# Mask products before or after the score products, chosen by what TensorE ran last

## The chip, the cores and the metric

The kernel runs on one core of a Trainium2 chip. The metric is the device time of one execution, in microseconds (us); lower is better. A core has five engines that work side by side and meet through semaphores: PE (TensorE, matrix products), DVE (VectorE), ACT (ScalarE), POOL (GpSimd) and SP (SyncE, which here issues the DMA transfers). The profile has a sixth column, PEld: the loads of the stationary operand, which overlap PE's products.

## The reference

Two attentions follow each other. The first has 8 batches of 8 heads, 576 positions, 64 features, and keeps only the 32 largest scores of each row:

```python
scores = scale * np.matmul(q, k.transpose(0, 1, 3, 2))
kth = np.partition(scores, -top_k, axis=-1)[..., -top_k:-top_k + 1]
scores = np.where(scores >= kth, scores, -1000000000.0)
attn = softmax(scores)                      # with 1e-9 added to the sum
x = np.matmul(attn, v)                      # heads side by side: (8, 576, 512)
```

The second (the MoE stage) takes `x`, picks 2 of 4 experts for each position by a gate, and lets each expert do a causal attention with its own projections:

```python
q, k, v = x @ wq[e], x @ wk[e], x @ wv[e]
a = softmax(where(causal, -1e9, scale * (q @ k.T)))
out += gate[:, e] * (a @ v @ wo[e])
```

## The kernel before

**Tiling.** Two heads form a pair, so a batch is four pairs and the program has 32 of them. The 2 x 576 query rows of a pair are cut into nine tiles of 128 rows, numbered `j`: 0 to 3 belong to the first head (operands `opa`), 5 to 8 to the second (`opb`), and tile 4 holds the 64 left-over rows of each.

**The first attention.** For each group of three tiles PE makes the scores (`scores`, float32r products, L554), ACT copies them to SBUF (`copy`, tile `s`, L558), and DVE finds the 32 largest of each row in a chain of maxima (`f1` to `f5`, `win`, `rep`, L568 to L609). ACT then makes a mask from the scores and the 32nd value (`mask`, bf16, L649): zero for what is kept, positive for what isn't. `stats` (L674) turns the row's maximum and its sum into four rows of numbers; PE transposes them (`s8`, tile `stat`, L723) and ACT writes them into the operands (`s9`, L727).

Then the scores are made a second time, transposed, with keys on the partitions. This is the task `st` (L752). It has two parts that add up in one PSUM tile of two banks: `product` makes four float32r products (128 x 128 stationary; 256 and 320 columns, twice), the second pair of which reads the extended operand `k2a` or `k2b`; then `piece` multiplies each of five mask tiles with a bf16 matrix that holds a huge negative number on its diagonal (`negi`), which pushes the scores that are not kept far down. There are eight such tasks in a pair, and a ninth, `j == 4`, with eight products and ten or eleven mask pieces. ACT takes the exponential (`exp`, tile `pt`, L799), and PE multiplies the result with the values (`av`, L769): float32 products whose stationary operand is only 64 columns wide, two side by side in the array. The first product of a PSUM bank is issued with `start=True`, the others add to it.

**The MoE stage** of a batch runs spread out between the pairs of the following batch: projections (`proj`, `vproj`, float32r), scores for five row tiles (`s_stage`, L1015), a row maximum on DVE (`m_stage`), the exponential on ACT (`e_stage`), transposes on PE (`t_stage`, L1048), the product with the values (`avm`), and the output projection (`prod`). For the first four row tiles, `s_stage` first puts the causal mask into PSUM (`identb` and `tri`, bf16, full array), then adds three pairs of products `qk` whose contraction has 64 rows, two side by side.

**Order of issue.** No engine's order is written by hand. Every piece of work is added to a `Plan` as a task with an engine, an estimated duration, its predecessors, its buffers and a priority. `Plan.order` (L144) plays the tasks through: for each engine it takes, among the tasks whose estimated start lies within `SLACK` nanoseconds of the earliest, the one with the smallest priority, and advances that engine's clock. The priority is a due number, counted in pairs, plus a constant for the task's name (`BIAS`) and an offset for its stage (`D_...`). The program is issued in the order that comes out. Rings of buffers bound how far the engines run apart: three PSUM tiles (`SLOT`), one accumulator (`ACC`), 14 masks, one `raw`.

PE's tasks also have a kind (L99). The plan carries one flag, `short`, which says how the last PE task ended:

```python
            if t.kind:
                if short and t.kind not in (SHORT, TURN):
                    dur += self.SWITCH
                t.first = short
                short = t.kind in (SHORT, MIXED) or t.kind == EITHER and not short
```

`SWITCH` is 107 ns. `LONG` is float32r work (scores, projections), `SHORT` is float32 work and transposes (`av`, `avm`, `t_stage`, `s8`, `c4`). In the kernel before, `st` is `MIXED` (starts with float32r, ends with bf16), `s_stage` is `TURN` for the first four row tiles; no task is `EITHER`, and `t.first` is set but read by nobody.

Of the kernel before, what the change touches and what calls it, by code (L numbers as in the profile page):

```python
# [19 lines left out]
P = 128  # L20
TOPK = 32
OFF = (0, 64)
BASE = (0, 64)
# [75 lines left out]
LONG, SHORT, EITHER, MIXED, TURN = 1, 2, 3, 4, 5  # L99


class Plan:
# [5 lines left out]
           ("POOL", "SP"): 1400.0, ("DVE", "SP"): 1400.0, ("PE", "SP"): 1400.0}  # L108

    PORT = ("f1", "f3", "f4", "s1", "s7", "ot", "constants", "sub", "low_again")  # L110
    SLACK = 48.1507
    GAP = 160.0


# [123 lines left out]
def pool(n):  # L238
# [2 lines left out]

PEF = 1.0

BIAS = {"<lambda>": 21.16406, "again": 7.086664, "av": 0.291422, "avm": 7.96669, "c1": 6.060996, "c2": -16.917509, "c3":
        -25.219518, "c4": 7.40449, "c5": -35.33028, "cast": 16.673692, "cast_swap": -11.231639, "check1":
        -20.549209, "check2": 47.362819, "check3": -38.010145, "compare": 10.37121, "constants": 3.77208,
        "copy": -5.244973, "count": 19.276636, "diag": 12.150313, "dup": -0.574571, "dup1": -16.263021, "dup2":
# [4 lines left out]
        "load_swap": -1.709559, "loadv": -1.18649, "low_again": -15.590234, "m_stage": -34.500069, "mark":  # L252
        10.382567, "mask": -4.199012, "neg": 9.127403, "neg2": -15.174664, "o_stage": -15.926681, "oh":
        -11.134218, "ol": 20.300811, "ot": -22.486721, "prod": 24.66927, "proj": 0.24706, "rep": -3.538618,
        "s1": -38.259631, "s2": -18.732471, "s3": -11.549524, "s4": -14.828572, "s6": -6.937403, "s7": 7.577078,
        "s8": -2.208531, "s9": -18.824699, "s_stage": 0.053481, "scores": -0.261279, "st": -0.017376, "store":
        -19.029398, "sub": 10.142028, "t_stage": -1.573227, "tails": 9.736612, "vproj": 1.204296, "win":
        18.47031, "xh": 7.127005, "xl": 10.21211}
D_K2 = 29.144853
D_PREP = 2.849825  # L260
D_SC = 0.543928
D_TIE = 11.578646
D_MASK = 1.607309
D_STAT = -3.592427
D_TAIL = 0.282302
D_STEP = 0.102808
D_MOE = 4.208214
D_LAST = 5.999043
D_PEN = 4.17838
D_SPAN = 4.144087  # L270
MP = (14,3)
STO = (0, 1, 5, 2, 6, 3, 7, 8, 4)

# [2 lines left out]
def kernel(ctx, tc, qk, vL, wq, wk, wv, wo, out):  # L276
# [13 lines left out]
    def mm(o, l, r, start=False, stop=False):  # L290
        nc.tensor.matmul(o, l, r, start=start, stop=stop, skip_group_check=True)  # L291
# [107 lines left out]
    pl = Plan()  # L399
    add = pl.add  # L400
    lo, hi, al = slice(0, 64), slice(64, 128), slice(0, 128)
# [30 lines left out]
    def parts_of(j):  # L432
        return [(x, REST[x]) for x in range(2)] if j == 4 else [rows_of(j)]
# [80 lines left out]
        w.v = add("SP", 910, lambda: nc.sync.dma_start(w.vt.t, vL[b, i]), bufs=[w.vt], prio=3, tag="loadv")  # L514
        return w

    def product(sl, o0, split, ops, ls, rs, stop):

        k = 0
        for x, r, t in ops:  # L520
            for l, rr in zip(ls, rs):
                for c0, c1 in halves(split):
                    mm(sl[:, o0 + c0:o0 + c1], t[l][:, r], t[rr][:, OFF[x] + c0:OFF[x] + c1], start=(k == 0),
                       stop=stop and k == 2 * len(ops) - 1)
                k += 1
# [218 lines left out]
    def tail(w, shift, xb):  # L744
        acc = Buf(ACC)

        def piece(sl, prt, o0, split, c0, c1, lhsT, r):
            for a, z in ((c0, min(c1, split)), (max(c0, split), c1)):
                if a < z:
                    mm(sl[prt, o0 + a:o0 + z], lhsT, negi[:, r + a - c0:r + z - c0])  # L750

        def st(j, sl):  # L752
            split = SPLIT[0] if j < 4 else SPLIT[1]
            o0 = 512 - split
            product(sl.t, o0, split, parts(w, j), (1, 3), (0, 2), False)
            for x, r in parts_of(j):
                if j == 4:
                    prt = slice(64 * x, 64 * x + 64)
                    kc = slice(512, 576) if x == 0 else slice(0, 64)
                else:  # L760
                    prt = al
                    kc = slice(r.start - OFF[x], r.stop - OFF[x])
                c0 = 512 if x == 0 else 0
                piece(sl.t, prt, o0, split, c0, c0 + 64, w.mask[4].t[:, kc], 64 * x)
                for t in range(4):
                    c0 = BASE[x] + t * P
                    piece(sl.t, prt, o0, split, c0, c0 + P, w.mask[t + 5 * x].t[:, kc], 0)

        def av(j, pts):  # L769
            v = w.vt.t  # L770
# [13 lines left out]
        for j in STO:  # L784
            pl.due = w.p + D_TAIL + D_STEP * len(es)
            sl = Buf(SLOT)
            pt = ptb[j] = Buf(PT)
            x = 0 if j < 4 else 1
            o0 = 512 - (SPLIT[0] if j < 4 else SPLIT[1])
            need = [shift[x], w.k2d[x]] + (w.masked[0:5] if j < 4 else w.masked[4:9])  # L790
            if j == 4:
                need = shift + w.masked + w.k2d
            elif j > 4:
                need.append(shift[0])
            mb = w.mask if j == 4 else (w.mask[0:5] if j < 4 else w.mask[4:9])
            a = add("PE", 767 if j != 4 else 1500, lambda j=j, sl=sl: st(j, sl), need, bufs=[sl, pt] + used(w, j, True) + mb, prio=2, tag="st",
                    kind=MIXED)
            w.last_st.append(a)
            es[j] = add("ACT", act(S), lambda sl=sl, pt=pt, o0=o0: nc.scalar.activation(  # L799
                pt.t, sl.t[:, o0:o0 + S], AF.Exp, scale=0.125), [a], bufs=[sl, pt], prio=1, tag="exp")  # L800
        a = None
        for j in (0, 1, 2, 3, 4):
# [3 lines left out]
            a = add("PE", 1020 if j != 4 else 790, lambda j=j, pts=pts: av(j, pts), [es[k] for k in jj] + [w.v, a],  # L806
                    bufs=pts + [acc, w.vt], prio=1, tag="av", kind=SHORT)
# [6 lines left out]
        a = add("PE", 250, neg, [c], bufs=[acc, xb], prio=1, kind=LONG)  # L814
# [8 lines left out]
    def moe(b, p, xbs, xdone, wd, span, final):  # L823
        v = nc.vector
        v2, gg, ot = Buf(V2), Buf(G), Buf(OT)
# [39 lines left out]
        for t in range(5):  # L865
            sl = Buf(SLOT)
# [93 lines left out]
        for gp in range(2):  # L960
# [6 lines left out]
            for name, k in (("q", 0), ("k", 2)):  # L967
                sl = Buf(SLOT)
                o0 = 512 - 288
# [41 lines left out]
            for t in (0, 1, 2, 3, 4):  # L1011
# [3 lines left out]
                def s_stage(t=t, w=w, sl=sl, qk=qk, bd=bd):  # L1015
                    qh, ql, kh, kl = qk.t
                    if t < 4:
                        for h in range(2):
                            mm(sl.t[:, 512 * h + t * P:512 * h + w], identb, tri, start=True)
                        for n, (l, rr) in enumerate(((qh, kh), (ql, kh), (qh, kl))):  # L1020
                            for h in range(2):
                                r = slice(64 * h, 64 * h + 64)
                                mm(sl.t[:, 512 * h:512 * h + w], l[r, t * P:(t + 1) * P], rr[r, 0:w], stop=(n == 2))
# [47 lines left out]
                a = add("ACT", n * act(w, True, 1, 1), e_stage, [a], bufs=[sl, sm, pr], prio=2)  # L1071
                exps.append(a)
# [64 lines left out]
        split = []  # L1137
# [74 lines left out]
    t = add("PE", 100, check2, [t], bufs=[fin])  # L1212
    add("DVE", 100, check3, [t], bufs=[fin])
    for t in pl.order():
        t.fn()


    again = nc.values_load(flag, min_val=0, max_val=1)
    with tc.If(again > 0):
        for x in range(2):  # L1220
            blank(nc.vector, x, 0)
        blank_later()
        marks.clear()
        with tc.For_i(0, B) as b:
            pl.restart()
            batch(b, 0, {n: [] for n in "vqko"}, True)
            for t in pl.order():
                t.fn()


# [42 lines left out]
```

## Time and profile before

| what | value |
|---|---|
| time, median of 3 runs | 1211.62 us (1210.65 to 1213.2) |
| time of the profiled execution | 1211.31 us |
| its span, first to last instruction | 1209.5 us |
| granted TensorE clock, mean | 0.976 |
| PE busy | 1125.3 us, 93% of the span |
| DVE busy | 1096.4 us, 91% |
| ACT busy | 986.6 us, 82% |
| POOL busy | 378.4 us, 31% |

A row of the profile names a line of the kernel, an engine, an operation, and the tiles it writes and reads, `out<-in`, with the shape. All of `mm`'s products have the line L291, so the tiles tell them apart: `slot<-opa,opa` is a score product, `slot<-opa,k2a` the second pair of a `st`, `slot<-negi,mask` a mask product, `acc<-pt,vt` is `av`, `slot<-tri,identb` the causal mask, `slot<-qk,qk` the MoE scores. In the timeline a row begins with the start and the length of a run of such instructions, ends with their count, and has in square brackets how long the engine was idle before it and whose work ended that. PE's products are pipelined: the next begins before the one before has ended, so lengths overlap, and the distance from one start to the next is what a product takes of PE's time.

### The profile page before, as it was taken

How to read it: one execution, taken by the hardware profiler on the slowest of the kernel's cores; microseconds unless marked ns; L12 is line 12 of the kernel's file. 1: busy time of each engine (PE TensorE's matmuls, PEld its weight loads, DVE VectorE, ACT ScalarE, POOL GpSimd, SP SyncE). 2: the span in 40 equal slices, each digit the busy share in tenths (PEclk: the TensorE clock that was granted, in tenths of full speed). 3: DMA queues.
4: the chain of work that ended last, by engine and by line, in shares of the span. 5: the costliest groups of instructions: out<-in, count | busy, mean ns of one | idle time of the engine just before them, and what ended most of it. 6: DMA issues, size and time to landing. Idle time of an engine off the chain costs nothing. (4 is left out here: it accounts for less than half of the span.)

```text
span 1209.5 us, 28181 instructions
## 1 busy us (share of the span) xinstructions
PE 1125.3 (93%) x9330; PEld 923.2 (76%) x9330; DVE 1096.4 (91%) x4745; ACT 986.6 (82%) x2050; POOL 378.4 (31%) x803
## 2 busy tenths in 40 slices
PE   3578789999999999999999999999999999999997
PEld 3456668887878778887888878787788878787785
DVE  7999999999999999999999999999999999999121
ACT  5677678899898988979888988989888898888554
POOL 4422222424224332333224232243323333242112
PEclk8688899999999999999999999999999999999999
DMA  7132322224432333333422234323332334220101
GB/s 200 43 90 74 98 74 61 74 72 108 112 86 71 88 90 78 81 91 91 114 81 66 60 98 112 91 66 91 105 76 68 86 99 121 66 71 11 47 5 43
DMA packets 45578, 98.56 MB, mean 81 GB/s; under 512 B 7792, under 2 KB 7792, under 8 KB 45424
## 3 DMA queue, kind: packets, MB, share of 16 engines
q1 hardware_dynamic: 45424, 96.67, 30.0%
q8 instruction: 76, 1.25, 0.4%
q14 instruction: 78, 0.64, 0.2%
HBM read 32.06 MB, written 9.44 MB: 34 GB/s over the span
## 5 line engine op out<-in xcount | busy, mean ns | idle before, releaser
L799 ACT ACTIVATE pt<-slot 128x576 f32<-128x576 f32 x288 | 186.4, 650 | 89.9 <-PE slot L291 88.3
L649 ACT ACTIVATE mask<-s,top 128x576 bf16<-128x576 f32 x288 | 216.4, 772 | 10.6 <-DVE top L603 10.0
L291 PE MATMUL slot<-opa,opa 128*128 128x256 f32 (+3 forms) x984 | 196.1, 326 | 25.1 <-ACT s L558 15.3
L291 PE MATMUL acc<-pt,vt 128*64 128x256 f32 (+3 forms) x1152 | 199.6, 423 | 1.9 <-ACT pt L799 1.9
L291 PEld LDWEIGHTS slot<-opa,opa 128*128 128x128 f32 (+1 forms) x984 | 146.1, 197 | 64.1 <-issue 24.3
L291 PE MATMUL slot<-opb,opb 128*128 128x320 f32 (+1 forms) x960 | 185.7, 314 | 5.9 <-ACT pt L799 2.1
L590 POOL COPY scrap<-cand 128x1 f32<-128x1 f32 x96 | 18.1, 189 | 534.9 <-DVE cand L586 528.3
L558 ACT ACTIVATE s<-slot 128x576 f32<-128x576 f32 x288 | 174.3, 652 | 10.1 <-PE slot L291 9.0
L291 PEld LDWEIGHTS slot<-opb,opb 128*128 128x128 f32 x960 | 141.3, 193 | 22.2 <-issue 11.0
L603 DVE MAX8 top<-cand 128x8 f32<-128x168 f32 x576 | 152.3, 319 | 0.0
L291 PEld LDWEIGHTS acc<-pt,vt 128*64 128x64 f32 (+1 forms) x1152 | 94.5, 143 | 49.8 <-issue 16.3
L577 DVE MAX8 cand<-fb 128x8 f32<-128x288 f32 x288 | 130.4, 453 | 0.0
L291 PE MATMUL slot<-negi,mask 128*128 128x128 bf16 (+3 forms) x1632 | 129.8, 218 | 0.0
L569 DVE TENSOR_TENSOR fa<-s 128x864 f32<-128x864 f32 x96 | 102.7, 1070 | 17.2 <-ACT s L558 16.3
L572 DVE TENSOR_TENSOR fb<-s 128x864 f32<-128x864 f32 x96 | 100.9, 1051 | 0.0
L629 POOL TENSOR_TENSOR ind<-cand,top 128x513 bf16<-128x513 f32 x96 | 100.7, 1049 | 0.1
L291 PEld LDWEIGHTS <-mask 128*128 128x128 bf16 (+1 forms) x1632 | 80.0, 102 | 24.5 <-issue 5.2
L603 DVE MAX8 top<-oct 128x8 f32<-128x72 f32 x576 | 93.6, 216 | 0.0
L608 DVE MATCH_REPLACE8 cand<-top,cand 128x168 f32<-128x168 f32 x288 | 88.6, 317 | 0.0
L637 ACT ACTIVATE ind<-ind,tiny 128x513 bf16<-128x513 bf16 (+1 forms) x96 | 69.7, 726 | 14.3 <-POOL ind L632 7.1
L723 PE MATMUL slot<-identf,stat 128*4 128x128 f32 x288 | 43.1, 278 | 35.6 <-DVE stat L719 28.0
L291 PE MATMUL slot<-opa,k2a 128*128 128x256 f32 (+1 forms) x320 | 70.1, 301 | 1.5 <-ACT opa L727 1.5
(192 smaller groups left out, 2505.9 us busy)
## 6 DMA issues: line engine op xcount, KB each, us to landing
raw<-in_qk_dram SPq DMA_DIRECT2D x31, 576.0 KB, 4.1
opa<-raw SPq DMA_DIRECT2D x93, 144.0 KB, 2.4
opb<-raw SPq DMA_DIRECT2D x93, 144.0 KB, 2.5
vt<-in_vL_dram SPq DMA_DIRECT2D x32, 320.0 KB, 3.1
opa<-opa SPq DMA_DIRECT2D x62, 144.0 KB, 2.4
opb<-opb SPq DMA_DIRECT2D x62, 144.0 KB, 2.9
out_dram<-pr SPq DMA_DIRECT2D x32, 256.0 KB, 2.0
k2a<-opa SPq DMA_DIRECT2D x32, 144.0 KB, 2.3
```

What stands on the lines that cost most here:

```text
L291: nc.tensor.matmul(o, l, r, start=start, stop=stop, skip_group_check=True)
L558: nc.scalar.activation(s3.t[:, n], sl.t[:, o0:o0 + S], AF.Copy)
L569: v.tensor_tensor(out=fa.t, in0=s3.t[:, :, 0:288], in1=s3.t[:, :, 288:576], op=OP.max)
L572: v.tensor_tensor(out=fb.t, in0=s3.t[:, :, 0:288], in1=s3.t[:, :, 288:576], op=OP.min)
L577: v.max(out=c.t[:, n, 160:168], in_=fb.t[:, n])
L603: v.max(out=w.top.t[0][:, j, 8 * r:8 * r + 8], in_=oc.t[:, n] if r < 2 else c.t[:, n, 0:168])
L608: v.match_replace(out=c.t[:, n, 0:72] if r == 1 else src, in_values=src, imm_value=LOW, in_to_replace=w.top.t[0][:, j, 8 * r:8 * r + 8])
L629: nc.gpsimd.tensor_tensor(out=ind.t[:, 0:513].rearrange("p (a n) -> p a n", a=3), in0=c.t, in1=m32[:, js[0]:js[0] + 3, 31:32].to_broadcast ...
L637: nc.scalar.activation(ind.t[:, 0:n], ind.t[:, 0:n], AF.Sign, bias=tiny, accum_out=signs[:, 3 * w.p + g:3 * w.p + g + 1])
L649: nc.scalar.activation(w.mask[j].t, s3.t[:, n], AF.Relu, bias=w.top.t[0][:, j, 31:32], scale=-1.0)
L723: nc.tensor.transpose(sl.t[0:4, j * P:(j + 1) * P], ft(parts()[2][:, j]), identf)
L799: es[j] = add("ACT", act(S), lambda sl=sl, pt=pt, o0=o0: nc.scalar.activation(pt.t, sl.t[:, o0:o0 + S], AF.Exp, scale=0.125), [a], bufs=[s ...
```

## The change

`st` for the eight full tiles, and `s_stage` for the first four row tiles, get the kind `EITHER`. When such a task is issued, `pl.first` holds the plan's flag for it. If PE's preceding work ended short, the bf16 mask products come first and the float32r products last; otherwise the products come first and the masks last. Whichever part comes first opens the PSUM banks with `start=True`; `piece` keeps a list of the banks that are still to be opened. `j == 4` keeps products first. The duration of `s_stage` in the plan falls by 107 ns, which is now added by `SWITCH` where it applies. The constants of the planner (`SLACK`, `BIAS`, the `D_...` offsets) have new values throughout, so the order in which every engine's work is issued is another. The diff, with most of the constants left out:

```diff
-    SLACK = 48.1507
+    SLACK = 37.3701
...
-        "s8": -2.208531, "s9": -18.824699, "s_stage": 0.053481, "scores": -0.261279, "st": -0.017376, "store":
-        -19.029398, "sub": 10.142028, "t_stage": -1.573227, "tails": 9.736612, "vproj": 1.204296, "win":
...
+        "s8": 1.999852, "s9": -21.590516, "s_stage": 0.100849, "scores": -0.260385, "st": -0.105205, "store":
+        -17.808275, "sub": 10.647924, "t_stage": -5.807017, "tails": 2.016157, "vproj": 1.227239, "win":
...
-D_PREP = 2.849825
-D_SC = 0.543928
...
-D_MOE = 4.208214
...
+D_PREP = -3.645945
+D_SC = 0.556526
...
+D_MOE = 4.203192
...
-    def product(sl, o0, split, ops, ls, rs, stop):
+    def product(sl, o0, split, ops, ls, rs, stop, start=True):
...
-                    mm(sl[:, o0 + c0:o0 + c1], t[l][:, r], t[rr][:, OFF[x] + c0:OFF[x] + c1], start=(k == 0),
+                    mm(sl[:, o0 + c0:o0 + c1], t[l][:, r], t[rr][:, OFF[x] + c0:OFF[x] + c1], start=start and k == 0,
...
-        def piece(sl, prt, o0, split, c0, c1, lhsT, r):
+        def piece(sl, prt, o0, split, c0, c1, lhsT, r, fresh=()):
             for a, z in ((c0, min(c1, split)), (max(c0, split), c1)):
                 if a < z:
-                    mm(sl[prt, o0 + a:o0 + z], lhsT, negi[:, r + a - c0:r + z - c0])
+                    bank = a >= split
+                    mm(sl[prt, o0 + a:o0 + z], lhsT, negi[:, r + a - c0:r + z - c0], start=bank in fresh)
+                    if bank in fresh:
+                        fresh.remove(bank)
 
         def st(j, sl):
             split = SPLIT[0] if j < 4 else SPLIT[1]
             o0 = 512 - split
-            product(sl.t, o0, split, parts(w, j), (1, 3), (0, 2), False)
...
+            def prods(first):
+                product(sl.t, o0, split, parts(w, j), (1, 3), (0, 2), False, first)
+
+            def masks(first):
+                fresh = [False, True] if first else []
+                for x, r in parts_of(j):
...
+                    piece(sl.t, prt, o0, split, c0, c0 + 64, w.mask[4].t[:, kc], 64 * x, fresh)
+                    for t in range(4):
+                        c0 = BASE[x] + t * P
+                        piece(sl.t, prt, o0, split, c0, c0 + P, w.mask[t + 5 * x].t[:, kc], 0, fresh)
+            order = (masks, prods) if pl.first and j != 4 else (prods, masks)
+            order[0](True)
+            order[1](False)
...
-                    kind=MIXED)
+                    kind=EITHER if j != 4 else MIXED)
...
                 def s_stage(t=t, w=w, sl=sl, qk=qk, bd=bd):
                     qh, ql, kh, kl = qk.t
                     if t < 4:
...
+                        def causal(first):
                             for h in range(2):
...
+                                mm(sl.t[:, 512 * h + t * P:512 * h + w], identb, tri, start=first)
+
+                        def prods(first):
...
+                        order = (causal, prods) if pl.first else (prods, causal)
+                        order[0](True)
+                        order[1](False)
...
-                pe = (690, 690, 923, 1095, 920)[t]
+                pe = (583, 583, 816, 988, 920)[t]
...
-                        kind=TURN if t < 4 else MIXED)
+                        kind=EITHER if t < 4 else MIXED)
...
     for t in pl.order():
+        pl.first = t.first
         t.fn()
```

More of the change, by code (lines that the diff above doesn't have):

```diff
@@ L242 @@
 PEF = 1.0
[L244 to L247, printed above, removed]
[4 rows of a table removed]
[L252 to L255, printed above, removed]
-        "s8": -2.208531, "s9": -18.824699, "s_stage": 0.053481, "scores": -0.261279, "st": -0.017376, "store":
-        -19.029398, "sub": 10.142028, "t_stage": -1.573227, "tails": 9.736612, "vproj": 1.204296, "win":
-        18.47031, "xh": 7.127005, "xl": 10.21211}
@@ L259 @@
-D_K2 = 29.144853
-D_PREP = 2.849825
-D_SC = 0.543928
[L262 to L266, printed above, removed]
-D_MOE = 4.208214
-D_LAST = 5.999043
-D_PEN = 4.17838
-D_SPAN = 4.144087
+BIAS = {"<lambda>": 31.116457, "again": 5.625849, "av": 0.3831, "avm": 8.589162, "c1": 13.314437, "c2": -25.695809,
+        "c3": -22.825654, "c4": 3.760134, "c5": -37.850449, "cast": 24.507043, "cast_swap": -8.915878, "check1":
+        -18.153406, "check2": 51.514065, "check3": -33.987139, "compare": 23.809938, "constants": 13.545533,
+        "copy": -0.595107, "count": 21.688419, "diag": 17.455247, "dup": -3.324263, "dup1": -13.285251, "dup2":
[4 rows of a table added]
+        "load_swap": 0.6639, "loadv": 0.664296, "low_again": -17.322237, "m_stage": -42.425271, "mark":
+        9.399599, "mask": -0.627829, "neg": 2.848053, "neg2": -9.627095, "o_stage": -12.802777, "oh":
+        -17.352957, "ol": 19.932502, "ot": -27.700052, "prod": 32.000557, "proj": 0.291373, "rep": -6.363904,
+        "s1": -35.079154, "s2": -11.540778, "s3": -9.618098, "s4": -15.183134, "s6": -3.496027, "s7": -0.019881,
+        "s8": 1.999852, "s9": -21.590516, "s_stage": 0.100849, "scores": -0.260385, "st": -0.105205, "store":
+        -17.808275, "sub": 10.647924, "t_stage": -5.807017, "tails": 2.016157, "vproj": 1.227239, "win":
+        12.708734, "xh": 4.071972, "xl": 9.135895}
@@ L271 @@
+D_K2 = 38.296512
+D_PREP = -3.645945
+D_SC = 0.556526
+D_TIE = 16.158892
+D_MASK = 1.311812
+D_STAT = -3.623497
+D_TAIL = 0.326443
+D_STEP = 0.097738
+D_MOE = 4.203192
+D_LAST = 10.779732
+D_PEN = 4.153693
+D_SPAN = 4.107641
 MP = (14,3)
@@ L754, in st @@
             o0 = 512 - split
-            product(sl.t, o0, split, parts(w, j), (1, 3), (0, 2), False)
[L756 to L767, printed above, removed]
+            def prods(first):
[3 more added lines that the diff above has]
+                for x, r in parts_of(j):
+                    if j == 4:
+                        prt = slice(64 * x, 64 * x + 64)
+                        kc = slice(512, 576) if x == 0 else slice(0, 64)
+                    else:
+                        prt = al
+                        kc = slice(r.start - OFF[x], r.stop - OFF[x])
+                    c0 = 512 if x == 0 else 0
+                    piece(sl.t, prt, o0, split, c0, c0 + 64, w.mask[4].t[:, kc], 64 * x, fresh)
[5 more added lines that the diff above has]
+            order[1](False)
         def av(j, pts):
@@ L1017, in s_stage @@
                     if t < 4:
-                        for h in range(2):
-                            mm(sl.t[:, 512 * h + t * P:512 * h + w], identb, tri, start=True)
-                        for n, (l, rr) in enumerate(((qh, kh), (ql, kh), (qh, kl))):
+                        def causal(first):
                             for h in range(2):
-                                r = slice(64 * h, 64 * h + 64)
-                                mm(sl.t[:, 512 * h:512 * h + w], l[r, t * P:(t + 1) * P], rr[r, 0:w], stop=(n == 2))
+                                mm(sl.t[:, 512 * h + t * P:512 * h + w], identb, tri, start=first)
+                        def prods(first):
+                            for n, (l, rr) in enumerate(((qh, kh), (ql, kh), (qh, kl))):
+                                for h in range(2):
+                                    r = slice(64 * h, 64 * h + 64)
+                                    mm(sl.t[:, 512 * h:512 * h + w], l[r, t * P:(t + 1) * P], rr[r, 0:w],
+                                       start=first and n == 0, stop=(n == 2))
+                        order = (causal, prods) if pl.first else (prods, causal)
+                        order[0](True)
+                        order[1](False)
                     else:
@@ L1227 @@
             for t in pl.order():
+                pl.first = t.first
                 t.fn()
```

8 rows, old and new, of the table BIAS are left out of this document.

## The prediction

> **What bounds the kernel now.** I began with the page's busy times.
>
> ```profile
> span 1209.5 us, 28181 instructions
> ...
> PE 1125.3 (93%) x9330; PEld 923.2 (76%) x9330; DVE 1096.4 (91%) x4745; ACT 986.6 (82%) x2050; POOL 378.4 (31%) x803
> ```
>
> Two engines are nearly full, so a mean share decides nothing. The trace repeats itself once per batch, so I next took stretches: the ramp, one repeat, and the last MoE.
>
> ```profile
> 0.00:240.00 240.00, 184.20 (x1297) 145.50 (x1298) 225.68 (x1007) 176.44 (x342) 75.40 (x155) 0.89 0.33 89
> 422.18:561.86 139.68, 137.14 (x1168) 113.32 (x1167) 136.12 (x589) 121.56 (x256) 45.69 (x97) 1.00 0.33 87
> 1120.00:1209.50 89.50, 78.17 (x674) 64.96 (x672) 13.85 (x30) 44.79 (x101) 15.70 (x38) 0.98 0.09 31
> ```
>
> The columns are stretch, length, and then busy time of PE, PEld, DVE, ACT and POOL. In a repeat of 139.68 us, PE is busy for 137.14 and DVE for 136.12: PE can give at most 3.56 us per repeat before DVE alone fills it. In the ramp PE is idle for 55.8 us of 240; at the end PE works almost alone.
>
> Which of the two leads changes within a repeat. The timeline at the moments where one engine had to wait:
>
> ```profile
> 422.18 1.06 DVE L569 TENSOR_TENSOR fa<-s 128x864 f32<-128x864 f32 x1 [1.72 <-ACT s L558]
> 429.25 0.27 PE L723 MATMUL slot<-identf,stat 128*4 128x128 f32 x1 [0.74 <-DVE stat L719]
> 499.64 0.16 DVE L885 COPY v<-slot 128x4 f32<-128x4 f32 x1 [0.43 <-ACT v L882]
> 524.17 0.27 PE L723 MATMUL slot<-identf,stat 128*4 128x128 f32 x1 [0.81 <-DVE stat L719]
> 561.86 1.06 DVE L569 TENSOR_TENSOR fa<-s 128x864 f32<-128x864 f32 x1 [1.72 <-ACT s L558]
> ```
>
> DVE waits for scores that PE made (422.18, 561.86) or for a projection (499.64); PE waits for DVE's statistics (429.25, 524.17). From the end of a PE wait to the next DVE wait, PE is on the path: 429.25 to 499.64 and 524.17 to 561.86, 108.1 us or 77% of a repeat. Only there does a shorter PE stream shorten the span.
>
> **The change, price by price.** A `st` task has four float32r products and five bf16 mask products; the number of tasks is the number of 64-wide mask products:
>
> ```profile
> L291 PE MATMUL slot<-negi,mask 128*128 128x64 bf16 x256 | 52.7, 206 | 0.0
> ```
>
> No instruction is added or removed; the 256 tasks keep their matmuls and weight loads, and only what stands beside what changes. So I price borders, from start to start. First a `st` behind float32r work:
>
> ```profile
> 607.54 0.43 PE L291 MATMUL slot<-opb,opb 128*128 128x320 f32 x2
> 607.81 0.43 PE L291 MATMUL slot<-opb,k2b 128*128 128x320 f32 x2
> ```
>
> Its first pair takes 607.81 - 607.54 = 0.27 us. Next, two `st` behind an attention product (`av`):
>
> ```profile
> 432.98 1.19 PE L291 MATMUL acc<-pt,vt 128*64 128x256 f32 x8
> 434.10 0.53 PE L291 MATMUL slot<-opa,opa 128*128 128x256 f32 x2
> 434.47 0.42 PE L291 MATMUL slot<-opa,k2a 128*128 128x256 f32 x2
> 434.74 0.43 PE L291 MATMUL slot<-negi,mask 128*128 128x64 bf16 x5
> 434.97 0.51 PE L291 MATMUL slot<-opb,opb 128*128 128x320 f32 x2
> 435.32 0.43 PE L291 MATMUL slot<-opb,k2b 128*128 128x320 f32 x2
> 435.59 0.43 PE L291 MATMUL slot<-negi,mask 128*128 128x64 bf16 x5
> 435.82 1.64 PE L291 MATMUL slot<-wo,qk 128*128 128x512 f32 x6
> ```
>
> Behind `av` the first pair takes 434.47 - 434.10 = 0.37, so that border costs 0.10. Behind masks it takes 435.32 - 434.97 = 0.35, so 0.08; but the five masks before it last 434.97 - 434.74 = 0.23 instead of 0.26 (475.71 to 475.97 below, masks before bf16), which leaves 0.05. Going from products to masks costs nothing: the second pair, 434.47 to 434.74, takes the same 0.27.
>
> The trace of before has no mask product right behind `av`; this decides the case. The nearest bf16 row behind narrow tiles is the causal product behind row-tiled `qk`:
>
> ```profile
> 475.71 0.43 PE L291 MATMUL slot<-negi,mask 128*128 128x64 bf16 x5
> 475.97 0.28 PE L291 MATMUL slot<-tri,identb 128*128 128x128 bf16 x2
> 476.18 0.55 PE L291 MATMUL slot<-qk,qk 64*128 64x128 f32 x6
> 476.66 0.28 PE L291 MATMUL slot<-tri,identb 128*128 128x128 bf16 x2
> 476.87 0.62 PE L291 MATMUL slot<-qk,qk 64*128 64x256 f32 x6
> ```
>
> The two causal products take 0.21 behind masks and 0.21 behind `qk`: nothing is added. The other nearest row is a float32 transpose behind `av`:
>
> ```profile
> 402.42 1.19 PE L291 MATMUL acc<-pt,vt 128*64 128x256 f32 x8
> 403.54 0.44 PE L1053 MATMUL slot<-identf,pr 128*128 128x128 f32 x2
> 403.73 0.36 PE L291 MATMUL slot<-opa,opa 128*128 128x256 f32 x1
> ...
> 418.19 1.04 PE L1053 MATMUL slot<-identf,pr 128*128 128x128 f32 x8
> 419.06 0.71 PE L1057 MATMUL slot<-identf,pr 128*128 128x128 f32 x5
> 419.52 0.36 PE L291 MATMUL slot<-opa,opa 128*128 128x256 f32 x1
> ```
>
> Two transposes take 0.19 there. Undisturbed, thirteen take 1.33 with the last showing some 0.03, so a step is about 0.11, two would take 0.14, and 0.05 is added. The border from `av` to masks thus costs 0 to 0.05, and 0.10 if masks fare no better than products. I take 0.01, by the bf16 row.
>
> Both fences show 1.12 us from the start of `av` to whatever comes next: 432.98 to 434.10 and 402.42 to 403.54. The Trainium skill (TensorEngine Tiling (Array Packing), Tiling Modes, Key Properties) says that a change of tiling mode drains TensorE. That speaks against the change, and the trace agrees: the emptying is paid before products and before transposes alike. If the drain were the whole price of the border, masks first would gain nothing there, the second rival below.
>
> How many borders: along PE's rows of the timeline a `st` comes directly behind `av` 85 times; the first and the last of them:
>
> ```profile
> 56.87 0.53 PE L291 MATMUL slot<-opa,opa 128*128 128x256 f32 x2
> ...
> 1137.54 0.53 PE L291 MATMUL slot<-opb,opb 128*128 128x320 f32 x2
> ```
>
> All 85 turn to masks first: 85 x (0.10 - 0.01) = 7.7 us less. A masks-first task pays its mask-to-product border inside itself, while the one behind it, now products first, pays none. Replaying the toggle on the old sequence of tasks, mask-to-float32r borders go from 192 to 208: 16 x 0.05 = 0.8 more. Where a `st` follows transposes (31 times) I count nothing, the transposes being full-array work like what follows. Of the 64 `s_stage` tasks, 23 change sides; each arrangement goes once into row tiles and once out, and what differs is a step of 0.05 to 0.10 either way: 23 x (-0.05 to +0.09), -1.2 to +2.1; I take -0.3. Sum for PE: -7.7 + 0.8 - 0.3 = **-7.2 us**; with 0 for masks behind `av` and the better s_stage end -9.0, with 0.05 and the worse end -1.4, with 0.10 up to +2.9.
>
> On the path: of the 85 borders, 17 lie before 240 us, 64 in the repeats, 4 after 1120. Repeats: 7.2 x 64/85 = 5.4, of which 77% is 4.2. Ramp: 1.4, of which I count a quarter, 0.35, as PE is idle there anyway. End: 0.34 at PE's 87% share, 0.3. Together 4.85 us.
>
> Masks first puts the four products, and all that follows in PE's queue, behind the wait for ACT's masks. I set the first `st` of each half of a pair against the end of the last mask it reads; the shortest lead in a repeat is this one:
>
> ```profile
> 424.88 1.45 ACT L649 ACTIVATE mask<-s,top 128x576 bf16<-128x576 f32 x2
> 430.89 0.43 PE L291 MATMUL slot<-opb,k2b 128*128 128x320 f32 x2
> ```
>
> The masks end at 424.88 + 1.45 = 426.33, and the second pair of products starts at 430.89: over 4 us, which hide the wait, so I cost it at nothing. With that lead gone a task could lose the 2 x 0.27 = 0.54 us of products that now run ahead of its masks, and ACT's exponential, `av` and the scores behind it would wait as long.
>
> The new order moves everything else. The plan takes 107 ns for a border that my rows price at 0 to 0.10 us; on the old sequence it would count 464 - 341 = 123 borders fewer, 13.2 us, against my 7.2. So it hands out PE time that PE doesn't have, and some hand-overs to ACT and DVE will come later than planned; what that costs is inside the rivals. By the numbers in the code most ranks on an engine stay as they are; the one I take seriously is `t_stage` on PE, rival four. Loads and duplicates on SP get later due numbers, but `raw` has a single buffer, so its load starts when that frees, whatever its rank; the three duplicates behind it follow ACT's cast and POOL's subtraction as before. I cost it at nothing; if a load came late, the cast, the duplicates and then the scores would be late, which is a wait of the second rival's kind.
>
> **The rivals.** *Second: nothing that can be measured.* The border from `av` costs masks 0.10 too, or ACT's and DVE's waits take the rest back. Then PE's sum is near zero: 1211.0. For it: the same 1.12 us behind every `av`. Against it: the 0.21 row.
>
> *Third: much faster.* The new order also drops part of the repeated waits. The floor is DVE's work, 139.68 - 136.12 = 3.56 us in each of (1120 - 240)/139.68 = 6.3 repeats, 22 us; half of it gives 1211.3 - 11 = 1200.3. For it: the waits sit at the same place in every repeat, so one better order removes them all. Against it: every wait answers to two engines that are both 97% busy.
>
> *Fourth: slower.* `t_stage` ranked on PE at 4.21 - 1.57 = 2.6 past its batch's first pair, and scores of the next batch's first pair near 4 - 0.54 - 0.26 = 3.2; now it is 4.20 - 5.81 = -1.6 against 3.2, so transposes go ahead of any scores that could start with them. Eight cost 419.06 - 418.19 = 0.87 us, and the wait at 422.18 shows what that does: thirteen stand ahead of the scores, and DVE then waits 1.72. Two more such places per repeat cost 2 x 0.87 x 6.3 = 11.0: 1206.4 + 11.0 = 1217.4. It decides from (4.9 + 2.4)/6.3 = 1.16 us per repeat on. Against it: ranks count only among tasks that can start within 37 ns of each other.
>
> **How the numbers follow.** The profiled run took 1211.31 us, 0.3 below the median of 1211.62. 1211.3 - 4.9 = **1206.4**. Chances: forecast 0.45 (its own range 1203 to 1209), nothing 0.22, much faster 0.18, slower 0.15. No change is within 0.2%, 2.4 us, about what a measurement of this kernel can tell. Faster: 0.18 plus nearly all of the forecast, 0.61; same: most of the second and a little of the first, 0.24; slower 0.15. The range, 1199 to 1214, leaves out the far parts of the third and fourth.
>
> **What would show it.** Right: masks directly behind `av` with a first step no longer than elsewhere, and four products of 0.27 + 0.27 behind a products-first task; PE busy near 136.3 in a repeat; repeats near 139.0. Wrong: the masks behind `av` stretched by 0.05 or more; PE shorter but the waits of PE for `stat` grown by as much; or DVE's wait for `s` longer than 1.72, or at more places, behind transposes.

## The result, and the profile after

The changed kernel takes 1190.41 us (median of 4 runs, 1189.86 to 1193.28) against 1211.13 us: the ratio is 0.9836, with a 95% interval of 0.9819 to 0.9853. It is faster by 20.7 us, four times what the prediction forecast, and outside its range.

The profiled execution took 1193.28 us. The changed kernel's page, busy times:

```profile
span 1191.4 us, 28234 instructions
...
PE 1118.2 (94%) x9330; PEld 918.3 (77%) x9330; DVE 1084.2 (91%) x4745; ACT 988.5 (83%) x2050; POOL 367.3 (31%) x803
```

PE's busy time fell by 1125.3 - 1118.2 = 7.1 us; the prediction's sum for PE was 7.2. That the two agree here is luck, as the experiments show. DVE's busy time fell as well, by 12.2 us, although DVE executes the same 4745 instructions on the same shapes. That wasn't in the prediction at all.

The same three kinds of stretch as before (ramp, one repeat, last MoE); the columns are stretch, length, and busy time of PE, PEld, DVE, ACT, POOL:

```profile
0.00:240.00 240.00, 187.16 (x1362) 149.21 (x1363) 229.18 (x1036) 183.84 (x356) 77.11 (x161) 0.91 0.35 93
479.69:617.66 137.97, 136.72 (x1169) 113.06 (x1168) 135.03 (x590) 121.92 (x256) 44.40 (x97) 1.00 0.33 88
1103.40:1191.40 88.00, 76.56 (x643) 63.83 (x639) 13.21 (x30) 42.87 (x96) 12.89 (x33) 0.96 0.09 29
```

A repeat is 1.71 us shorter (139.68 to 137.97). PE is now busy for 99% of it. The 136.12 us of DVE work that the prediction took for a floor have become 135.03.

The waits at the ends of a repeat, from the timeline of the changed kernel:

```profile
479.69 1.06 DVE L569 TENSOR_TENSOR fa<-s 128x864 f32<-128x864 f32 x1 [0.65 <-ACT s L558]
485.87 0.39 PE L291 MATMUL slot<-opa,opa 128*128 128x256 f32 x1 [0.37 <-DVE v L896]
522.22 0.33 PE L291 MATMUL slot<-ptm,v 128*64 128x128 f32 x2 [0.23 <-ACT s L558]
617.66 1.06 DVE L569 TENSOR_TENSOR fa<-s 128x864 f32<-128x864 f32 x1 [0.66 <-ACT s L558]
```

DVE's longest wait for scores is 0.66 instead of 1.72, and PE's waits of 0.74 and 0.81 for DVE's statistics are gone.

To see where in the run the time went I used DVE's group maxima (line 569), 96 in every kernel, as milestones. From the 19th to the 91st DVE does the same 72 groups, three double batches, in every kernel; I call this the middle. The middle of the kernel before, and of the changed one, in the columns of above:

```profile
208.56:1047.60 839.04, 823.01 (x6998) 680.03 (x6997) 816.66 (x3534) 729.35 (x1531) 275.40 (x582) 1.00 0.33 87
```

```profile
204.96:1031.62 826.66, 817.18 (x6978) 675.21 (x6977) 807.11 (x3535) 728.53 (x1527) 265.14 (x580) 1.00 0.33 87
```

Of the 18.2 us of span, 12.4 are gained here, 3.6 before it (208.56 against 204.96) and 2.2 behind it. In the middle PE's busy time is shorter by 5.8 and DVE's by 9.6. The 3.6 us in front of the middle can't be put down to the order alone: up to the 19th group the granted clock was 0.87 before and 0.89 after, and the five variants of the old order below get there after 206.68 to 210.57 us, at clocks of 0.84 to 0.90. In the middle it is 1.00 in both kernels, so the middles can be compared.

The length of the middle is PE's busy time and its idle time, so the other 6.6 of the 12.4 us are idle time, 16.0 before and 9.5 after. The largest of PE's waits in the middle of before, with its total, how often it came, and the longest:

```profile
PE slot L723 <- DVE stat L719: 9.2, 12, 0.8
```

In the middle of the changed kernel there is none of these.

Which operations of DVE became shorter? The groups by form, of before:

```profile
L569 DVE TENSOR_TENSOR fa<-s 128x864 f32<-128x864 f32 x96 | 102.7, 1070 | 17.2 <-ACT s L558 16.3
...
L579 DVE TENSOR_TENSOR cand<-fa 128x432 f32<-128x432 f32 x96 | 63.5, 662 | 0.0
...
L719 DVE TENSOR_TENSOR stat<-stat,stat 128x4 fp32r<-128x4 f32 x32 | 16.8, 526 | 1.6 <-ACT stat L715 1.5
...
L689 DVE TENSOR_TENSOR stat<-top 128x128 f32<-128x128 f32 x32 | 14.5, 454 | 1.1
...
L719 DVE TENSOR_TENSOR stat<-stat,stat 128x5 fp32r<-128x5 f32 x32 | 5.4, 168 | 0.0
```

and of the changed kernel:

```profile
L569 DVE TENSOR_TENSOR fa<-s 128x864 f32<-128x864 f32 x96 | 109.8, 1143 | 8.5 <-ACT s L558 8.5
...
L579 DVE TENSOR_TENSOR cand<-fa 128x432 f32<-128x432 f32 x96 | 57.6, 600 | 0.0
...
L689 DVE TENSOR_TENSOR stat<-top 128x128 f32<-128x128 f32 x32 | 10.1, 317 | 1.1
...
L719 DVE TENSOR_TENSOR stat<-stat,stat 128x4 fp32r<-128x4 f32 x32 | 9.6, 302 | 0.6 <-ACT stat L715 0.6
```

Not all became shorter: the group maxima (L569) went from 1070 to 1143 ns. But an operation on four elements a partition (L719) took 526 ns in the mean, and takes 302; its twin on five elements, which meets POOL less, took 168 before. Nothing in it changed; what stands beside it did. One of the long ones, in the timeline of before, with POOL's row of the same moment:

```profile
427.69 1.42 DVE L719 TENSOR_TENSOR stat<-stat,stat 128x4 fp32r<-128x4 f32 x1
427.66 1.43 POOL L471 TENSOR_TENSOR raw<-raw,opa 128x576 f32<-128x576 f32 x1
```

DVE's small operation starts with POOL's long one and ends with it, at 429.11. PE's wait of 0.74 us that the prediction shows at 429.25 is a wait for this very operation; six of the twelve waits above come behind one that took 1.41 to 1.43 us. I summed, over the four groups above and their near relatives, what each operation took beyond its undisturbed length (L719: 0.16 us): 25.7 us in the kernel before, and in nearly every case a POOL operation overlaps it; 14.4 us in the changed one. The sum depends by about 1 us on what is taken for undisturbed. This standing still is counted as busy time. The Trainium skill (GPSIMD Engine Reference, Specifications) says that POOL shares its SBUF interfaces with VectorE and that they get in each other's way when a DVE instruction has two SBUF inputs. The trace agrees: the operations that became longer are TENSOR_TENSOR with two inputs, and a maximum with one input (MAX8, L603, `top<-cand`) takes 319 ns in both kernels.

### The profile page after: what moved, and what is told of

It reads as the page before. It is cut to its first block, busy times and chain, and to the rows that moved or that the text cites. A ratio compares the mean times of both kernels' runs of the same rounds, so it can differ in the third digit from the quotient of the medians.

```text
span 1191.4 us, 28234 instructions
## 1 busy us (share of the span) xinstructions
PE 1118.2 (94%) x9330; PEld 918.3 (77%) x9330; DVE 1084.2 (91%) x4745; ACT 988.5 (83%) x2050; POOL 367.3 (31%) x803
## 5 line engine op out<-in xcount | busy, mean ns | idle before, releaser
L291 PE MATMUL slot<-opa,opa 128*128 128x256 f32 (+3 forms) x984 | 198.7, 324 | 22.3 <-ACT s L558 10.5
L649 ACT ACTIVATE mask<-s,top 128x576 bf16<-128x576 f32 x288 | 213.0, 771 | 7.3 <-DVE top L603 6.7
L590 POOL COPY scrap<-cand 128x1 f32<-128x1 f32 x96 | 18.2, 190 | 624.6 <-DVE cand L586 593.5
L291 PE MATMUL acc<-pt,vt 128*64 128x320 f32 (+3 forms) x1152 | 199.1, 419 | 3.5 <-ACT pt L810 3.5
L558 ACT ACTIVATE s<-slot 128x576 f32<-128x576 f32 x288 | 176.3, 653 | 20.7 <-PE slot L291 19.2
L291 PE MATMUL slot<-opb,opb 128*128 128x320 f32 (+1 forms) x960 | 183.1, 312 | 7.3 <-DMA opb<-raw 4.8
L291 PEld LDWEIGHTS slot<-opb,opb 128*128 128x128 f32 x960 | 144.6, 194 | 14.2 <-DMA opb<-raw 5.2
L603 DVE MAX8 top<-cand 128x8 f32<-128x168 f32 x576 | 152.3, 319 | 0.0
L291 PE MATMUL slot<-negi,mask 128*128 128x128 bf16 (+3 forms) x1632 | 125.7, 217 | 1.1 <-ACT opb L727 0.7
L569 DVE TENSOR_TENSOR fa<-s 128x864 f32<-128x864 f32 x96 | 109.8, 1143 | 8.5 <-ACT s L558 8.5
L603 DVE MAX8 top<-oct 128x8 f32<-128x72 f32 x576 | 93.6, 217 | 0.0
L291 PE MATMUL slot<-opb,k2b 128*128 128x320 f32 x320 | 70.5, 302 | 1.3 <-ACT opb L727 0.8
```

The source lines that it names most:

```text
L558: nc.scalar.activation(s3.t[:, n], sl.t[:, o0:o0 + S], AF.Copy)
L569: v.tensor_tensor(out=fa.t, in0=s3.t[:, :, 0:288], in1=s3.t[:, :, 288:576], op=OP.max)
L590: nc.gpsimd.tensor_copy(scrap[:, g:g + 1], c.t[:, 0, 143:144])
L603: v.max(out=w.top.t[0][:, j, 8 * r:8 * r + 8], in_=oc.t[:, n] if r < 2 else c.t[:, n, 0:168])
L649: nc.scalar.activation(w.mask[j].t, s3.t[:, n], AF.Relu, bias=w.top.t[0][:, j, 31:32], scale=-1.0)
```

## The experiments

Two theories stood against each other. *A*: the toggle itself makes the gain. *B*: the new order makes it, above all because DVE stands still less beside POOL, and the toggle is worth what the prediction gave it. In what follows, kernels that were measured together are compared in us, others by their ratios to the kernel before.

**Toggle and order apart.** The toggle can be switched without touching the order of a single instruction outside a task. First the new order with masks always last:

```diff
-            order = (masks, prods) if pl.first and j != 4 else (prods, masks)
+            order = (prods, masks)
...
-                        order = (causal, prods) if pl.first else (prods, causal)
+                        order = (causal, prods)
```

> The changed kernel's order of issue on every engine, but masks always last and the causal product always first, as before. Theory A (the toggle itself makes the gain, by shorter borders on PE): the gain goes, 1205 to 1211 us. Theory B (the new order makes the gain, by fewer DVE operations that stand still while POOL works; the toggle is worth the 5 us of the prediction at most): 1193 to 1198 us, with the sum of stretched two-input DVE operations near the 14 us of the changed kernel and PE busy some 7 us longer.

Then the old order, planned as before, with the toggle set afterwards from what PE runs:

```diff
+        short = False
+        for t in out:
+            if t.kind:
+                t.first = short
+                short = not short if t.swap else t.kind in (SHORT, MIXED)
         return out
```

> The order of issue of before on every engine; within each task masks first or last by what PE ran last, as in the change. Theory A: 1190 to 1197 us. Theory B: 1204 to 1208 us, PE busy some 7 us shorter than before, the sum of stretched DVE operations still above 20 us (before: 25.7).

The order alone: 1205.06 us, ratio 0.9952 (0.9935 to 0.9968). The toggle alone: 1208.31, ratio 0.9976 (0.9962 to 0.9989). Together they would add up to 0.993; the change has 0.9836. The first time is the one that *A* expected and the second is close to what *B* expected, so both theories fall as they stand. Alone, the toggle saves 0.24%, some 3 us; in the new order it saves 0.9952 - 0.9836 = 1.16%, some 14 us. More than half of the gain belongs to the two together.

The middle, for the order alone and for the toggle alone:

```profile
206.96:1042.13 835.17, 826.41 (x6975) 677.39 (x6974) 810.59 (x3534) 729.10 (x1527) 264.54 (x580) 1.00 0.32 86
```

```profile
210.57:1047.54 836.97, 818.24 (x7001) 679.70 (x6998) 816.61 (x3535) 729.28 (x1531) 275.37 (x582) 1.00 0.33 87
```

In the old order the toggle takes 823.01 - 818.24 = 4.8 us from PE and 2.1 from the length. In the new order it takes 826.41 - 817.18 = 9.2 from PE and 8.5 from the length. So there are two factors: the toggle saves PE almost twice as much, and nearly all of it comes through instead of less than half.

The first factor can be counted in part. In the middle, the toggle turns 60 borders from `av` or `avm` to the products of a `st` into other borders in the old order, and 81 in the new one; that is 1.35 times as many, for 1.9 times the saving. These borders also hide what the order is worth: without the toggle PE is busy for 826.41 - 823.01 = 3.4 us more in the new order than in the old one, while its idle time is down from 16.0 to 8.8 and its waits for `stat` are gone. So PE's 7.1 us in the whole run are a longer stream by the order and a larger saving by the toggle, and they match the forecast's 7.2 by luck. DVE's busy time shows what the order brings by itself, 816.66 to 810.59; the toggle takes 3.5 more from it in the new order (807.11) and nothing in the old one (816.61).

**The constants.** The change with the old planner constants, and the kernel before with the new ones:

> The change with the planner's constants (SLACK, BIAS, D_) of before: the plan knows the toggle, the weights are old, so the order is a third one. Theory A: 1190 to 1197 us. Theory B: the toggle's 3 to 5 us plus whatever the new order does to the DVE stalls; 1200 to 1215 us, and above 1206 if the stalls stay at 25 us.

> The kernel before with the planner's constants of the change: no toggle, a fourth order. Theory A: 1209 to 1213 us, as before. Theory B: it goes with the DVE stalls; 1195 to 1215 us, near 1200 only if their sum falls to 15 us.

1239.57 us (ratio 1.0235, 1.0213 to 1.0258) and 1242.30 us (1.0273, 1.0244 to 1.0302): both some 30 us slower than before, outside everything expected. The constants belong to the plan they were found for. In the last of these kernels DVE stands still beside POOL for only some 10 us, less than in the changed kernel, and it is the slowest: in its middle, 873.02 us, PE idles for 40.5 us and DVE for 67.6. Standing still alone doesn't decide, the engines' waits for each other do.

**Another order by one constant.**

> The changed kernel with one planner constant changed (SLACK 37.37 to 30); toggle and all else as in the change, another order. If the gain of the new order is a property of planning with the toggle, 1188 to 1195 us. If it belongs to this one order that was found, 1200 to 1240 us.

> The kernel before with one planner constant changed (SLACK 48.15 to 60). If orders with old weights are all alike, 1209 to 1214 us; if the order of before is itself one found among many, 1215 to 1245 us.

1207.15 us (0.9967, 0.9953 to 0.9981) and 1216.77 us (1.0039, 1.0027 to 1.0052). One constant, and the changed kernel loses some 16 us of its 21; the kernel before loses 5. The middle of the changed kernel with `SLACK` at 30:

```profile
205.86:1045.50 839.64, 817.69 (x6980) 675.55 (x6979) 808.40 (x3536) 728.82 (x1528) 268.73 (x582) 1.00 0.33 86
```

PE and DVE have almost the work of the changed kernel (817.18 and 807.11), yet the stretch takes 839.64 instead of 826.66: 13 us of waiting that no sum over one engine shows. Planning with the toggle is not enough for the gain; it came with this one order.

**Is POOL the cause of DVE's long operations, and do they cost time?** First I moved two of them from DVE to POOL for the second head of each pair, in the kernel before:

```diff
-            nc.vector.tensor_tensor(out=parts()[0], in0=m32[:, js], in1=m32[:, js, 0:1].to_broadcast([P, n, TOPK]),
+            (g if x == 1 else nc.vector).tensor_tensor(out=parts()[0], in0=m32[:, js], in1=m32[:, js, 0:1].to_broadcast([P, n, TOPK]),
...
-            nc.vector.tensor_tensor(out=hl[:, :, 3], in0=z[:, 1], in1=ft(hl[:, :, 2]), op=OP.subtract)
+            (g if x == 1 else nc.vector).tensor_tensor(out=hl[:, :, 3], in0=z[:, 1], in1=ft(hl[:, :, 2]), op=OP.subtract)
```

> Before, with two small DVE operations of each pair's second half (the subtraction of the row maximum and the 4-element remainder, lines 689 and 719) issued on POOL instead; order and masks as before. They hold 16.6 of the 25.7 us in which DVE stands still beside POOL, and some 14 us of DVE work. Theory B (DVE is full in the old order, PE has 16 us to spare between 208 and 1048 us): 1198 to 1206 us, then PE stops it. Theory C (DVE's standing still is slack, it would wait for scores otherwise): 1208 to 1213 us, and DVE's waits for the scores grow by what is freed.

1205.07 us (0.9953, 0.9937 to 0.9970), as B expected. Its middle:

```profile
206.68:1039.70 833.02, 820.52 (x6998) 679.91 (x6997) 798.10 (x3486) 728.80 (x1531) 318.22 (x629) 1.00 0.33 88
```

DVE is relieved of 816.66 - 798.10 = 18.6 us and the middle shortens by 6.0: a third comes through. But this edit also takes work away. The cleaner one keeps all work and all order, and cuts three long POOL operations into pieces (two of the three are shown):

```diff
-                    nc.gpsimd.tensor_tensor(out=raw.t[:, x], in0=raw.t[:, x], in1=ft(q2[:, c]), op=OP.subtract)
+                    for a in (0, 288):
+                        nc.gpsimd.tensor_tensor(out=raw.t[:, x, a:a + 288], in0=raw.t[:, x, a:a + 288],
+                                                in1=ft(q2[:, c.start + a:c.start + a + 288]), op=OP.subtract)
...
+                for a in range(3):
+                    nc.gpsimd.tensor_tensor(out=ind.t[:, 171 * a:171 * a + 171], in0=c.t[:, a],
+                                            in1=m32[:, js[a], 31:32].to_broadcast([P, 171]), op=OP.subtract)
```

> Before, with POOL's three long operations cut into pieces (line 471 into two, line 629 into three, line 1093 into two); same work, same order, nothing moved to another engine. If a DVE operation with two SBUF inputs stands still until the POOL instruction beside it has ended, shorter POOL instructions shorten the standing: the 25.7 us fall to some 10 to 15 us, DVE busy by 10 us, and the time by 2 to 6 us (moving two of the operations away gave 6): 1205 to 1209 us. If it is something else in DVE (its own queue, or PE's transfers), the stretched operations keep their lengths and the time stays at 1211 us, or gets worse by POOL's extra starts.

1204.82 us (0.9946, 0.9929 to 0.9962), a little better than expected. The groups by form (lines are shifted by two or three), POOL's pieces and DVE's operations:

```profile
L581 DVE TENSOR_TENSOR cand<-fa 128x432 f32<-128x432 f32 x96 | 60.1, 626 | 0.0
...
L472 POOL TENSOR_TENSOR raw<-raw,opa 128x288 f32<-128x288 f32 x62 | 49.2, 814 | 50.1 <-ACT opa L462 50.1
...
L692 DVE TENSOR_TENSOR stat<-top 128x128 f32<-128x128 f32 x32 | 12.0, 375 | 1.1
...
L722 DVE TENSOR_TENSOR stat<-stat,stat 128x4 fp32r<-128x4 f32 x32 | 11.8, 368 | 1.7 <-ACT stat L718 1.6
```

The operation on four elements fell from 526 to 368 ns, the others from 662 to 626 and from 454 to 375, though only POOL's instructions were touched; the twin on five elements rose from 168 to 234. The middle:

```profile
210.10:1041.60 831.50, 823.41 (x6998) 679.79 (x6997) 811.05 (x3534) 728.06 (x1531) 313.57 (x786) 1.00 0.33 88
```

DVE's busy time is down by 5.6, about half of the 10 that was expected, and the length by 7.5. The sum of the standing still comes to about 21 us, where 10 to 15 was expected. PE's wait for `stat`, which was 9.2 us, shows how the one leads to the other:

```profile
PE slot L726 <- DVE stat L722: 1.3, 6, 0.2
```

Shorter POOL instructions shorten DVE's standing still, and in the old order PE was waiting for it: PE's idle time falls from 16.0 to 8.1 us, 7.9 of it in this wait. POOL's own results come at other times too in this kernel, which the run doesn't keep apart.

**The same two edits on the changed kernel.**

> The changed kernel with the same two operations on POOL. Theory B: PE is full there (9.5 us idle between 205 and 1032 us), so DVE's relief of some 19 us brings at most 5: 1185 to 1191 us. Theory C: no change, 1190 us.

> The changed kernel with the same three POOL operations in pieces. PE has 9.5 us of idle time left between 205 and 1032 us, so at most a few us: 1186 to 1191 us if nothing falls out of step; 1195 to 1215 us if the order made for the old lengths no longer fits, as with the two operations moved to POOL.

The two operations on POOL: 1216.18 us (1.0039, 1.0028 to 1.0050), some 25 us slower than the changed kernel where a gain was expected. The pieces: 1194.50 (0.9858, 0.9841 to 0.9874), which the intervals don't tell from the changed kernel; no gain. The middle with the two on POOL, and its longest wait of DVE in a repeat:

```profile
209.90:1055.04 845.14, 821.68 (x6980) 675.71 (x6980) 796.80 (x3486) 729.23 (x1527) 310.24 (x631) 1.00 0.32 85
```

```profile
608.45 0.16 DVE L896 COPY v<-slot 128x4 f32<-128x4 f32 x1 [2.32 <-PE slot L291]
```

and the same wait in the changed kernel:

```profile
593.65 0.16 DVE L896 COPY v<-slot 128x4 f32<-128x4 f32 x1 [0.41 <-ACT mask L649]
```

DVE has 10 us less to do and waits 29 us more. In an order that is fixed in advance, an operation that comes a little later holds up everything issued behind it.

**Why the toggle pays more in the new order: is it because PE is full there?** I joined the toggle to the two kernels in which DVE had been relieved.

> The old order with the toggle and with the same two operations on POOL. Theory B: the toggle is worth more once DVE has room: 6 us or more against the run with the two operations alone (3.4 us in the old order without them); 1190 to 1199 us. Theory C: the two gains add or less than add, 1205 to 1209 us.

> The old order with the toggle and with POOL's three long operations in pieces. With the pieces alone PE is full (8 us idle of 831) as it is in the new order. If the toggle's worth depends on PE being full: 4 to 5 us less than the 1204.8 of the pieces alone, 1199.5 to 1201 us. If the toggle pays only where the order was planned with it: 2 us as in the old order otherwise, 1202 to 1204 us.

With the two on POOL: 1202.87 us (0.9929, 0.9912 to 0.9946), 2.2 less than without the toggle, where B expected 6 or more. With the pieces: 1200.60 (0.9916, 0.9894 to 0.9939), by the ratios 3.6 less than with the pieces alone (0.9946). That is nearest to the theory of the full PE, but the two intervals overlap. The middles, in that order:

```profile
209.65:1040.40 830.75, 815.32 (x7002) 679.61 (x6999) 798.09 (x3487) 729.17 (x1531) 318.53 (x629) 1.00 0.33 88
```

```profile
206.92:1036.30 829.38, 818.69 (x7000) 679.63 (x6997) 811.13 (x3534) 728.23 (x1531) 312.85 (x786) 1.00 0.33 88
```

The toggle takes 5.2 and 4.7 us from PE and 2.3 and 2.1 from the length of the middle, the same as in the old order without relief. In the execution with the pieces the middle begins at 206.92 instead of 210.10, a difference as large as those in front of the middle above. So a full PE is not what makes the toggle pay: with the pieces PE idled for only 8.1 us of the middle, with the new order for 8.8, and yet less than half came through there and nearly all here. With the pieces what was lost went into PE's transposes of `stat` again: their waits grew from 1.3 to 3.5 us, for 2.8 of which the profile names ACT's mask.

**Which borders carry the toggle.** In the new order, masks first behind `av` or `avm` alone (shown), and the counterpart, in which only a `st` behind them has its products first. In the first the causal products always come first; in the second they keep the change's toggle.

```diff
+        last = None
+        for t in out:
+            if t.eng == "PE":
+                t.first = last in ("av", "avm")
+                last = t.tag
```

> The changed kernel's order on every engine; masks first only where the work on PE directly before was an attention product (av, avm); everywhere else products first, and causal products first. If the border behind av carries the toggle's worth, as the prediction's sum has it (7.7 of 7.2 us): 1189 to 1194 us. If borders elsewhere carry it: 1198 to 1205 us, near the run without the toggle.

> The changed kernel's order; a task directly behind av or avm has its products first, every other task as in the change: the counterpart to the run with masks first behind av alone. If the two parts add up, 1199 to 1201 us (that run kept 9.1 of the toggle's 14.7). If the borders elsewhere are worth nothing alone, 1204 to 1206 us.

1196.02 us (0.9870, 0.9854 to 0.9887), slower than the 1189 to 1194 expected, and 1203.84 (0.9936, 0.9915 to 0.9957), again slower than expected. Against the order alone (0.9952) the borders behind `av` are worth 0.82%, the others 0.16%, both together 1.16%. The parts add up to 0.98%, which these intervals don't tell from 1.16%, nor the 0.16% from nothing. The middles agree: 835.17 us without the toggle, 828.38 with masks first behind `av` alone, 833.86 with them elsewhere, 826.66 with both. PE's busy time falls by 7.3 and 1.6 there, so in both most of it comes through. The border behind `av` carries most of it, as the prediction had it.

## Why the prediction was wrong

**The prices of the borders were right, but for one.** The undecided one, masks behind `av`, cost nothing. PE's timeline of the changed kernel:

```profile
498.57 1.19 PE L291 MATMUL acc<-pt,vt 128*64 128x256 f32 x8
499.69 0.42 PE L291 MATMUL slot<-negi,mask 128*128 128x64 bf16 x5
499.93 0.51 PE L291 MATMUL slot<-opa,opa 128*128 128x256 f32 x2
500.28 0.43 PE L291 MATMUL slot<-opa,k2a 128*128 128x256 f32 x2
500.54 0.43 PE L291 MATMUL slot<-opb,opb 128*128 128x320 f32 x2
500.81 0.43 PE L291 MATMUL slot<-opb,k2b 128*128 128x320 f32 x2
501.08 0.43 PE L291 MATMUL slot<-negi,mask 128*128 128x64 bf16 x5
```

The emptying behind `av` is the same 1.12 us, the five masks take 0.24, the first pair behind them 0.35, and all other pairs 0.26 or 0.27. It is so everywhere: 70 `st` stand right behind `av` in the middle, and their five masks take 0.235 to 0.237 us each time. The exception is a `st` behind transposes, which was counted at nothing: its first pair takes 0.35 in all 30 that stand so in the middle of before, 0.08 more than behind float32r work. PE's sum came out close all the same. The emptying, which the prediction held against the change, is paid in either arrangement, as before.

**PE's sum was right for the sequence it was made on.** With the old order the page shows PE busy 6.6 us shorter:

```profile
PE 1118.7 (93%) x9330; PEld 924.6 (76%) x9330; DVE 1099.5 (91%) x4745; ACT 986.7 (82%) x2050; POOL 379.7 (31%) x803
```

against 7.2 forecast (of the ends given for that sum, the better adds up to -8.9, not -9.0). On the path I counted 77% of the repeats' part, 4.85 us in all. Measured, the toggle alone gave a ratio of 0.9962 to 0.9989, 1.3 to 4.6 us: somewhat too high, since in the middle 2.1 of 4.8 came through (43%). The stretches from a wait of PE to a wait of DVE are no measure of what is on the path: of the 4.8 us that PE saved in the middle, 2.7 became idle time of PE (16.0 before, 18.7 with the toggle alone). The list of waits was not complete either: PE waits for 0.54 us at 493.27, longer than DVE's 0.43 at 499.64, in the midst of a stretch that was counted as PE's own.

**The step that failed: "replaying the toggle on the old sequence of tasks".** The prediction costed the new order at nothing in its forecast and left it to the rivals. The runs: the order alone is worth 0.48%, some 6 us, and it makes the same toggle worth 1.16%, some 14 us, instead of 0.24%. In the middle it ends PE's waits of 9.2 us for `stat`, and it has 81 instead of 60 borders for the toggle to work on.

**A second one: "PE can give at most 3.56 us per repeat before DVE alone fills it".** The third rival's floor took DVE's busy time for work. Of the 25.7 us by which some of its operations were longer than undisturbed, the change removed 11.3, and a repeat's DVE time went to 135.03. It could have been seen: the trace has four-element operations at 526 ns in the mean, and the wait for one of them, at 429.25, stands in the prediction. I didn't ask why it took so long.

**The rivals.** The third was the right one in kind, better order and shorter waits, with 0.18; its 1200.3 was still 10 us too slow, as it knew neither the standing still nor the joint effect. The fourth, transposes ahead of scores, didn't come: DVE's wait for scores fell to 0.65. The planner's credit of 107 ns a border, which I held against the change, did no harm that shows. No wait of PE for an ACT mask shows in a repeat of the changed kernel, so nothing speaks against the lead that the prediction relied on.

**What stays open.** Why nearly all of PE's saving comes through in the new order and less than half in the old one: DVE's room and PE's being full were tried and don't explain it; in the old order part of the saving turned into other waits of PE, but no run shows why those, and not others, are in the way. That the plan had the toggle's durations when it set the hand-overs is the remaining idea; the run with one constant changed shows only that a plan with the toggle can also lose most of the gain. Nor do more borders behind `av` need a plan that knows the toggle: the kernel before with `SLACK` at 60 has 71 in its middle, without it. And whether anything but the clock cut 3.6 us from the ramp is not shown.

## What to carry to other kernels

Where an order of issue is planned, a change of durations and the order made for them are one change: price the edit on the old sequence if you must, but give the new order a range of its own, which here was some 30 us for constants that don't fit and 16 us for one number. When two engines are both 97% busy, look inside the busy time: compare the mean of a group with the shortest of its kind before you call it work. And an improvement that frees one engine in a fixed order can cost more than it frees, so measure it in the order it is meant for.

## What was new about the hardware

A DVE operation with two SBUF inputs stood still until POOL's operation beside it had ended: four elements took 1.42 us beside a POOL subtraction of 1.43 us, and 0.16 us undisturbed. The profile counts that as busy time of DVE. Cutting POOL's 1.42 us operations into pieces of 0.81 brought the group's mean from 526 to 368 ns with no change on DVE. For PE: behind `av`, whose stationary operands are 64 columns wide, the first float32r pair took 0.10 us more and the first bf16 masks nothing more, on top of the same 1.12 us.
